# Image V in 384-column tiles, batch 0 first, with batch 1's x loaded between V's weight rows

## The chip, the cores and the metric

One core of a Trainium2 chip runs the whole program. The metric is the time of one execution on the device in microseconds (us); lower is better. "The same" means within 2% of the kernel before. All numbers below come from timed executions or from profiled ones. A profile is of a single execution.

## The reference

The program is one block of a diffusion transformer: two token streams, image and text, with joint attention. Everything is bf16.

```python
B, Ni, Nt, D = (2, 256, 32, 1152)
mod_i = (silu(c) @ wmod_img).reshape(B, 6, 1, D)      # shift, scale, gate: shi, sci, gai
hi = layernorm(x_img) * (1 + sci) + shi
qkvi = hi @ wqkv_img                                  # q, k, v of the image
# ... cut: the same for the text; joint softmax attention over 288 tokens ...
out_i = x_img + gai * (ai @ wo_img)
```

The part that matters here is the start: the layer norm of x, its transpose, the scale row `sci` (a matmul of `silu(c)` with a 2.65 MB weight), and image V. The kernel multiplies the normalized x by the scale and computes `V = (xn * (1 + sc)) @ Wv`; the shift's share of V is added later as a column.

## The kernel before

x is held as four tiles of 128 tokens: tiles 0 and 1 are batch 0, tiles 2 and 3 are batch 1. A weight of 1152 rows is held as 9 blocks of 128 rows, called rows 0 to 8 below (0.29 MB each). All these loads are issued to one DMA queue (`q1` of the page, with 39.85 of the 41.02 MB) in the order of the code. `pin` keeps an engine's instructions in program order. "Fillers" (`warm_up`) are matmuls of constants that keep TensorE busy while it waits.

```python
    ps_mm = ctx.enter_context(tc.tile_pool(name="ps_mm", bufs=6, space=PSUM))
    ps_tr = ctx.enter_context(tc.tile_pool(name="ps_tr", bufs=2, space=PSUM))

    # ... cut ...

    w_sc_i = wtile(0)
    w_v_i = wtile(1)
    sc_v, v_v = wview(wmod_img, D), wview(wqkv_img, 2 * D)
    for b in range(B):
        nc.sync.dma_start(x_i[:, b * TPB:(b + 1) * TPB, :], x_img[b].rearrange("(p t) d -> p t d", t=TPB))

    SCC = (0, 4, 7, K8, KT)
    for r0, r1 in zip(SCC, SCC[1:]):
        nc.sync.dma_start(w_sc_i[:, r0:r1, :], sc_v[:, r0:r1, :])
    for r0, r1 in ((0, 1), (1, 2), (2, 3), (3, 5), (5, 7), (7, KT)):
        nc.sync.dma_start(w_v_i[:, r0:r1, :], v_v[:, r0:r1, :])
    w_sh_i = load_w(2, wmod_img, 0)
    w_q_i = load_rows(3, wqkv_img, 0)
    w_sh_t = load_rows(0, wmod_txt, 0, (0, 1, 3, 6))
    nc.sync.dma_start(x_t[:], xt_flat[:, :])

    # ... cut ...

    xn_i = act.tile([P, NIT, D], bf, tag="A")
    hS_i = act.tile([P, KT, B * NI], bf, tag="Bt")
    xT_i = act.tile([P, KT, B * NI], bf)

    # ... cut ...

    sc_ps = ps_mm.tile([P, KT, LW], f32, tag="mm")

    def sc_rows(r0, r1):
        if r0 == 0:
            for g in range(NGG):
                mm(sc_ps[LW * g:LW * g + LW].rearrange("p c l -> p (c l)"), lhsT=unit[:], rhs=warm[:, 0:KT * LW],
                   start=True, stop=False, tile_position=(0, LW * g))
        for kt in range(r0, r1):
            for g in range(NGG):
                mm(sc_ps[LW * g:LW * g + LW], lhsT=sT32[:, kt, :], rhs=group(w_sc_i, kt, g),
                   start=False, stop=(kt == KT - 1), tile_position=(0, LW * g))

    def x_transposes(k0, b):
        tr_pool = b == 1 or k0 < 6
        tp = (ps_tr if tr_pool else ps_mm).tile([P, 3, NI], bf, tag="tr" if tr_pool else "mm", name="tp")
        for kt in range(k0, k0 + 3):
            for t in range(TPB):
                i = b * TPB + t
                tr(tp[:, kt - k0, t * P:(t + 1) * P], xn_i[:, i, kt * P:(kt + 1) * P], ident[:])
        dst = xT_i[:, k0:k0 + 3, b * NI:(b + 1) * NI]

        def copy_out():
            pin(nc.vector.tensor_copy(dst, tp[:]) if k0 == 3 else nc.scalar.copy(dst, tp[:]))

        return copy_out

    # ... cut ...

    VW = 512
    v_i = act.tile([P, NIT, D], bf, tag="A")
    accs = {}

    def v_open(ids, k0, k1, kt_major=True):
        for key in ids:
            if key not in accs:
                accs[key] = ps_mm.tile([P, VW], f32, tag="mm", name="vps")
        loop = [(kt, key) for kt in range(k0, k1) for key in ids] if kt_major else \
            [(kt, key) for key in ids for kt in range(k0, k1)]
        for kt, (i, cc) in loop:
            mm(accs[(i, cc)][:], lhsT=hS_i[:, kt, i * P:(i + 1) * P], rhs=w_v_i[:, kt, cc * VW:(cc + 1) * VW],
               start=(kt == 0), stop=(kt == KT - 1), skip_group_check=True)
            if kt == KT - 1:
                evac(v_i[:, i, cc * VW:(cc + 1) * VW], accs[(i, cc)][:])

    A0 = [(0, 0), (0, 1), (1, 0), (1, 1)]
    A1 = [(2, 0), (3, 0)]

    # ... cut ...

    s0 = ln_sums(x_i[:, 0, :], xn_i[:, 0, :])
    m1 = ln_stats(x_i[:, 1, :], P, between=silu_cols)
    ln_var(s0)
    ln_norm_dve(1, m1)
    ln_norm_act(0, s0)
    s2 = ln_sums(x_i[:, 2, :], xn_i[:, 2, :])
    m3 = ln_stats(x_i[:, 3, :], P)
    ln_var(s2)
    r3, r2 = ln_rstd(m3[:, 1:2], P), ln_rstd(s2[:, 2:3], P, sign=-1.0)
    ln_norm(x_i[:, 3, :], m3[:, 0:1], r3, P, xn_i[:, 3, :])
    ln_norm(x_i[:, 2, :], s2[:, 0:1], r2, P, xn_i[:, 2, :])
    for out in [x_transposes(k0, 0) for k0 in (0, 3, 6)]:
        out()
    sc_rows(0, 4)
    warm_up(3)
    sc_rows(4, 7)
    out01 = x_transposes(0, 1)
    out31 = x_transposes(3, 1)
    sc_rows(7, K8)
    sc_rows(K8, KT)
    out61 = x_transposes(6, 1)
    out01()
    sc_cols(0, 1)
    x_scale(0, 1, 0, step=1)
    sc_cols(1, 5)
    x_scale(1, 3, 0)
    v_open(A0, 0, 3)
    out31()
    out61()
    x_scale(0, 3, 1)
    sc_cols(5, KT)
    for k0 in (3, 6):
        for b in range(B):
            x_scale(k0, k0 + 3, b)
    v_open(A1, 0, 3)
    v_open(A0 + A1, 3, KT - 2)
    v_open(A0 + A1, KT - 2, KT, kt_major=False)

    # ... cut: mod_rows_of, 36 matmuls of 288 columns ...

    v_open([(2, 1)], 0, KT)
    p_sh = mod_rows_of(w_sh_i, sT32)
    sh_i = mod_cols_of(p_sh, "shc")
    nc.vector.tensor_copy(shT32[:, :, 0:B], sh_i[:, :, 0:B])
    # ... cut: h = xT * scale + shift in place, 18 operations on VectorE and ScalarE ...
    v_open([(3, 1)], 0, KT)

    def v_last():
        vps = ps_mm.tile([P, NIT, P], f32, tag="mm")
        for i in range(NIT):
            for kt in range(KT):
                mm(vps[:, i, :], lhsT=hS_i[:, kt, i * P:(i + 1) * P], rhs=w_v_i[:, kt, 2 * VW:D],
                   start=(kt == 0), stop=(kt == KT - 1))
        evac(v_i[:, :, 2 * VW:D], vps[:])

    # ... cut ...

    v_last()
    shift_v_rows()
    # ... cut: q and k projections, scores, softmax, attention, output projection ...
```

V is computed in tiles of 512, 512 and 128 columns. Six accumulators in PSUM, where the kernel's matmuls write their results, are open at once: four of batch 0 and two of batch 1; the rest follows later.

## Time and profile before

| | before |
|---|---|
| median of 6 runs | 118.44 us (118.32 to 118.53) |
| span of the profiled execution | 116.3 us |
| TensorE (PE) busy | 111.4 us, 96% |
| last scale row landed | 13.28 us |
| first V matmul | 14.31 us |
| first matmul of the q projection | 34.50 us |

From the profile page of the kernel before: the span, the engines' busy time, and two rows of the 40-slice table, where each digit is the busy share of one slice (2.9 us) in tenths. PEld is TensorE's weight load, DVE is VectorE, ACT is ScalarE, POOL is GpSimd.

```profile
span 116.3 us, 2500 instructions
...
PE 111.4 (96%) x1036; PEld 63.6 (55%) x1036; DVE 71.9 (62%) x151; ACT 44.9 (39%) x93; POOL 12.3 (11%) x34
...
PE   4999999999999999999999999999999999999990
...
DMA  4999999999999999999999999999999999932223
```

PE is full from the second slice to the last, and so is DMA until slice 35. Which of the two binds is told by the waits. The chain of waits of the kernel before follows the last instruction back to what released each step; columns are start in us, duration in us, and what it was.

```profile
11.15 0.75 PE wps L61 x3
11.90 0.51 PE sc_ps L61 x12
12.41 0.78 PE tp L64 x12
13.18 0.47 PE sc_ps L61 x8
...
13.68 0.23 DVE scc L257
...
14.00 0.27 DVE hS_i L264
...
14.31 13.77 PE vps L61 x63
28.08 1.22 PE gps L61 x36
29.30 4.06 PE vps L61 x45
33.36 1.22 PE gps L61 x36
34.57 19.53 PE ps L61 x90
```

Before 14.31 us PE is "busy" with fillers (`wps`) and with transposes of batch 1 (`tp`, 12 of 18 here) while the scale weights land. From 14.31 us on there is only real work, back to back: V (`vps`), the two modulation rows (`gps`), then the q projection (`ps`). From the first V matmul to the first q matmul it takes 34.50 − 14.31 = 20.19 us.

### The profile page before, as it was taken

To read this page: it belongs to the slowest core of one execution; us is meant where nothing else is said; L and a number is where in the kernel's file an instruction comes from. 1 tells how busy PE (TensorE), PEld (TensorE's weight loads), DVE (VectorE), ACT (ScalarE), POOL (GpSimd) and SP (SyncE) were. 2 spreads that over 40 slices of the span, in tenths; PEclk is the share of its full clock that TensorE was granted. 3 is DMA by queue.
4 is the path that set the end of the run, shared out by engine and by line. 5 is a ranking of instruction groups with operands and counts; after the bars stand their busy time and mean duration, and the time that the engine had idled before them with its cause. 6 is when DMAs were issued, how large, how long until landed. Compare 5 with 4: busy or idle time off the path is not lost.

```text
span 116.3 us, 2500 instructions
## 1 busy us (share of the span) xinstructions
PE 111.4 (96%) x1036; PEld 63.6 (55%) x1036; DVE 71.9 (62%) x151; ACT 44.9 (39%) x93; POOL 12.3 (11%) x34
## 2 busy tenths in 40 slices
PE   4999999999999999999999999999999999999990
PEld 1246544445574444445454457777866555666670
DVE  3468594063869999999995040017748666356671
ACT  4699710042752298825241233245747400100000
POOL 7300000000000000000000000004617000443000
PEclk9999999999999999999999999999999999999999
DMA  4999999999999999999999999999999999932223
GB/s 113 376 388 403 408 405 409 413 406 411 412 399 410 281 397 411 404 413 410 415 333 408 412 411 417 400 412 405 411 402 412 421 366 397 367 143 56 101 51 102
DMA packets 18917, 41.02 MB, mean 353 GB/s; under 512 B 1323, under 2 KB 1851, under 8 KB 18907
## 3 DMA queue, kind: packets, MB, share of 16 engines
q1 hardware_dynamic: 18032, 39.85, 89.5%
q0 software_dynamic: 480, 0.89, 2.3%
q10 hardware_dynamic: 395, 0.12, 0.4%
q8 instruction: 8, 0.13, 0.4%
q14 instruction: 2, 0.02, 0.0%
HBM read 39.52 MB, written 1.34 MB: 351 GB/s over the span
## 4 chain that ended last, share of the span: by engine, by line
PE 94%; DVE 3%; issue 0%; DVEq 0%
PE ps L61 52%; PE vps L61 15%; PE wps L61 7%; PE gps L61 5%; PE aps L61 5%; PE sps L61 5%; PE tp L64 2%; PE sc_ps L61 1%; DVE tmp L693 1%; PE pT_ps L64 1%; DVE o L694 1%; DVE warm L123 0%; PE tpt L64 0%; DVE hS_i L264 0%; DVE scc L257 0%
## 5 line engine op out<-in xcount | busy, mean ns | idle before, releaser
L61 PE MATMUL ps<-xT_i,t 128*128 128x512 bf16 x162 | 35.7, 379 | 0.0
L61 PEld LDWEIGHTS <-t 128*128 128x128 bf16 x324 | 20.5, 98 | 19.1 <-issue 0.7
L435 DVE SCALAR_TENSOR_TENSOR acc_sh<-t,sTf,acc_sh 128x1152 f32<-128x1152 bf16 x16 | 21.4, 1408 | 0.0
L61 PE MATMUL ps<-t,aT 128*128 128x384 bf16 (+3 forms) x153 | 20.3, 308 | 0.0
L61 PE MATMUL vps<-t,hS_i 128*128 128x512 bf16 (+1 forms) x108 | 17.9, 326 | 0.1
L61 PEld LDWEIGHTS <-aT 128*128 128x128 bf16 (+1 forms) x153 | 13.0, 101 | 7.1 <-issue 0.8
L61 PEld LDWEIGHTS <-hS_i 128*128 128x128 bf16 x108 | 9.0, 98 | 8.7 <-DVE hS_i L264 0.4
L365 ACT CAST qkT<-ps 128x512 bf16<-128x512 f32 (+2 forms) x11 | 6.1, 551 | 15.1 <-PE ps L61 13.7
L693 DVE TENSOR_TENSOR tmp<-ps,gb 128x384 bf16<-128x384 f32 (+2 forms) x13 | 6.8, 527 | 7.9 <-PE ps L61 7.9
L61 PE MATMUL wps<-warm 128*128 128x512 bf16 x25 | 8.7, 513 | 1.5 <-DVE unit L127 1.5
L580 POOL TENSOR_SCALAR pb<-e,rs 128x32 bf16<-128x32 f32 (+1 forms) x5 | 2.1, 414 | 74.7 <-DVE rs L577 74.6
L363 ACT ACTIVATE qkT<-ps 128x512 bf16<-128x512 f32 (+2 forms) x11 | 6.1, 561 | 8.6 <-PE ps L61 6.9
L180 DVE CAST v_i<-vps 128x512 bf16<-128x512 f32 x5 | 3.5, 692 | 7.5 <-PE vps L61 7.5
L565 DVE TENSOR_REDUCE nmx<-sps 128x1 f32<-128x288 f32 x4 | 1.8, 458 | 10.0 <-PE sps L61 10.0
L182 ACT CAST v_i<-vps 128x512 bf16<-128x512 f32 x4 | 2.3, 579 | 9.9 <-PE vps L61 9.9
L61 PEld LDWEIGHTS <-warm 128*128 128x128 bf16 x25 | 2.8, 122 | 5.8 <-issue 3.5
L61 PEld LDWEIGHTS <-sT 128*32 128x32 bf16 x180 | 4.6, 96 | 2.3 <-issue 1.6
L629 DVE TENSOR_SCALAR aT<-aps,svc 128x288 bf16<-128x288 f32 x9 | 4.3, 518 | 2.1 <-PE aps L61 2.1
L61 PE MATMUL sps<-qkT 128*128 128x288 bf16 (+1 forms) x54 | 5.5, 287 | 0.0
L61 PE MATMUL ps<-hT_t,t 128*128 128x64 bf16 x162 | 5.2, 193 | 0.1
L61 PE MATMUL gps<-t,sT 128*32 128x288 bf16 x144 | 5.2, 287 | 0.0
L61 PE MATMUL aps<-pT,v_i 128*128 128x288 bf16 x36 | 5.1, 287 | 0.0
(110 smaller groups left out, 105.3 us busy)
## 6 DMA issues: line engine op xcount, KB each, us to landing
t<-in_wqkv_txt_dram SPq DMA_DIRECT2D x3, 2592.0 KB, 19.2
t<-in_wmod_img_dram SPq DMA_DIRECT2D x2, 2592.0 KB, 14.0
t<-in_wmod_txt_dram SPq DMA_DIRECT2D x2, 2592.0 KB, 19.4
t<-in_wqkv_img_dram SPq DMA_DIRECT2D x3, 864.0 KB, 13.9
t<-in_wqkv_img_dram SPq DMA_DIRECT2D x1, 2592.0 KB
t<-in_wo_img_dram SPq DMA_DIRECT2D x3, 864.0 KB, 9.9
t<-in_wqkv_img_dram SPq DMA_DIRECT2D x3, 576.0 KB, 10.0
t<-in_wmod_txt_dram SPq DMA_DIRECT2D x2, 864.0 KB, 13.0
```

The source lines that it names most:

```text
L61: return pin(nc.tensor.matmul(*a, **k))
L64: return pin(nc.tensor.transpose(*a, **k))
L180: nc.vector.tensor_copy(out_ap, in_ap)
L182: nc.scalar.copy(out_ap, in_ap)
L363: nc.scalar.mul(out_ap, in_ap, SCALE)
L365: nc.scalar.copy(out_ap, in_ap)
L435: pin(nc.vector.scalar_tensor_tensor(acc, w_sh_t[:, kt, :], col, acc, op0=ALU.mult, op1=ALU.add))
L565: pin(nc.vector.reduce_max(nmx[0:qn, :], sps[0:qn, :], axis=AX.X, negate=True))
L580: pin(nc.gpsimd.tensor_scalar(pb[0:qn, NI + 2 * NT:NI + 3 * NT], e[0:qn, NI:NTOK], rs[0:qn, :], 0.0, op0=ALU.mult, op1=ALU.add))
L629: nc.vector.tensor_scalar(dst, tiles[(b, dt)][:], bias, None, op0=ALU.add)
L693: nc.vector.tensor_mul(tmp[:, 0:n], ps[:, 0:n], gb[:, b, c0:c0 + n])
L694: nc.vector.tensor_add(o[:, c0:c0 + n], tmp[:, 0:n], x_i[:, i, c0:c0 + n])
```

## The change

The intent: start V earlier and keep PE fed. The x of batch 1 no longer travels ahead of the scale weights, so the scale, and with it V, comes sooner. While V of batch 0 runs, batch 1's two x tiles arrive between the rows of V's weight, are normalized, and are transposed between V matmuls in two groups. The tiles of V become 384 columns wide, so that six accumulators hold exactly batch 0. In passing, the load of w_q is cut into two pieces instead of three.

The full diff:

```diff
--- before.py
+++ after.py
@@ -100,16 +100,18 @@
     w_sc_i = wtile(0)
     w_v_i = wtile(1)
     sc_v, v_v = wview(wmod_img, D), wview(wqkv_img, 2 * D)
-    for b in range(B):
-        nc.sync.dma_start(x_i[:, b * TPB:(b + 1) * TPB, :], x_img[b].rearrange("(p t) d -> p t d", t=TPB))
+    nc.sync.dma_start(x_i[:, 0:TPB, :], x_img[0].rearrange("(p t) d -> p t d", t=TPB))
 
     SCC = (0, 4, 7, K8, KT)
     for r0, r1 in zip(SCC, SCC[1:]):
         nc.sync.dma_start(w_sc_i[:, r0:r1, :], sc_v[:, r0:r1, :])
     for r0, r1 in ((0, 1), (1, 2), (2, 3), (3, 5), (5, 7), (7, KT)):
         nc.sync.dma_start(w_v_i[:, r0:r1, :], v_v[:, r0:r1, :])
+        if r0 in (1, 3):
+            i = TPB + r0 // 2
+            nc.sync.dma_start(x_i[:, i, :], x_img[1].rearrange("(p t) d -> t p d", t=TPB)[i - TPB])
     w_sh_i = load_w(2, wmod_img, 0)
-    w_q_i = load_rows(3, wqkv_img, 0)
+    w_q_i = load_rows(3, wqkv_img, 0, (0, 5))
     w_sh_t = load_rows(0, wmod_txt, 0, (0, 1, 3, 6))
     nc.sync.dma_start(x_t[:], xt_flat[:, :])
     w_k_i = load_w(4, wqkv_img, D)
@@ -211,7 +213,7 @@
     def ln_norm(x_ap, mean, rstd, np_, out_ap):
         pin(nc.vector.tensor_scalar(out_ap, x_ap, mean, rstd[0:np_, :], op0=ALU.subtract, op1=ALU.mult))
 
-    xn_i = act.tile([P, NIT, D], bf, tag="A")
+    xn_b = [act.tile([P, TPB, D], bf, tag="A%d" % b, name="xn%d" % b) for b in range(B)]
     hS_i = act.tile([P, KT, B * NI], bf, tag="Bt")
     xT_i = act.tile([P, KT, B * NI], bf)
 
@@ -225,7 +227,7 @@
         pin(nc.vector.transpose(t[:].rearrange("p c l -> p (c l)"), gps[:].rearrange("p c l -> p (c l)")))
         return t
 
-    sc_ps = ps_mm.tile([P, KT, LW], f32, tag="mm")
+    sc_ps = ps_tr.tile([P, KT, LW], f32, tag="tr")
 
     def sc_rows(r0, r1):
         if r0 == 0:
@@ -238,12 +240,10 @@
                    start=False, stop=(kt == KT - 1), tile_position=(0, LW * g))
 
     def x_transposes(k0, b):
-        tr_pool = b == 1 or k0 < 6
-        tp = (ps_tr if tr_pool else ps_mm).tile([P, 3, NI], bf, tag="tr" if tr_pool else "mm", name="tp")
+        tp = (ps_tr if b else ps_mm).tile([P, 3, NI], bf, tag="tr" if b else "mm", name="tp")
         for kt in range(k0, k0 + 3):
             for t in range(TPB):
-                i = b * TPB + t
-                tr(tp[:, kt - k0, t * P:(t + 1) * P], xn_i[:, i, kt * P:(kt + 1) * P], ident[:])
+                tr(tp[:, kt - k0, t * P:(t + 1) * P], xn_b[b][:, t, kt * P:(kt + 1) * P], ident[:])
         dst = xT_i[:, k0:k0 + 3, b * NI:(b + 1) * NI]
 
         def copy_out():
@@ -264,68 +264,67 @@
                 pin(nc.vector.tensor_scalar(hS_i[:, kt, t0:t1], xT_i[:, kt, t0:t1], sc1_i[:, kt, b:b + 1], None,
                                             op0=ALU.mult))
 
-    VW = 512
-    v_i = act.tile([P, NIT, D], bf, tag="A")
+    v_b = [act.tile([P, TPB, D], bf, tag="A%d" % b, name="v%d" % b) for b in range(B)]
     accs = {}
 
-    def v_open(ids, k0, k1, kt_major=True):
+    def v_open(ids, k0, k1, engines=None):
         for key in ids:
             if key not in accs:
-                accs[key] = ps_mm.tile([P, VW], f32, tag="mm", name="vps")
-        loop = [(kt, key) for kt in range(k0, k1) for key in ids] if kt_major else \
-            [(kt, key) for key in ids for kt in range(k0, k1)]
-        for kt, (i, cc) in loop:
-            mm(accs[(i, cc)][:], lhsT=hS_i[:, kt, i * P:(i + 1) * P], rhs=w_v_i[:, kt, cc * VW:(cc + 1) * VW],
+                accs[key] = ps_mm.tile([P, CH], f32, tag="mm", name="vps")
+        for kt, (i, cc) in [(kt, key) for kt in range(k0, k1) for key in ids]:
+            mm(accs[(i, cc)][:], lhsT=hS_i[:, kt, i * P:(i + 1) * P], rhs=w_v_i[:, kt, cc * CH:(cc + 1) * CH],
                start=(kt == 0), stop=(kt == KT - 1), skip_group_check=True)
             if kt == KT - 1:
-                evac(v_i[:, i, cc * VW:(cc + 1) * VW], accs[(i, cc)][:])
+                dst = v_b[i // TPB][:, i % TPB, cc * CH:(cc + 1) * CH]
+                if engines:
+                    pin((nc.scalar.copy if engines[ids.index((i, cc))] == "A" else nc.vector.tensor_copy)(
+                        dst, accs[(i, cc)][:]))
+                else:
+                    evac(dst, accs[(i, cc)][:])
 
-    A0 = [(0, 0), (0, 1), (1, 0), (1, 1)]
-    A1 = [(2, 0), (3, 0)]
+    V0, V1 = [[(i, cc) for i in range(b * TPB, (b + 1) * TPB) for cc in range(NCH)] for b in range(B)]
 
     def ln_norm_dve(i, mv):
-        ln_norm(x_i[:, i, :], mv[:, 0:1], ln_rstd(mv[:, 1:2], P), P, xn_i[:, i, :])
+        ln_norm(x_i[:, i, :], mv[:, 0:1], ln_rstd(mv[:, 1:2], P), P, xn_b[i // TPB][:, i % TPB, :])
 
     def ln_norm_act(i, sm):
-        ln_norm(x_i[:, i, :], sm[:, 0:1], ln_rstd(sm[:, 2:3], P, sign=-1.0), P, xn_i[:, i, :])
+        ln_norm(x_i[:, i, :], sm[:, 0:1], ln_rstd(sm[:, 2:3], P, sign=-1.0), P, xn_b[i // TPB][:, i % TPB, :])
 
-    s0 = ln_sums(x_i[:, 0, :], xn_i[:, 0, :])
+    s0 = ln_sums(x_i[:, 0, :], xn_b[0][:, 0, :])
     m1 = ln_stats(x_i[:, 1, :], P, between=silu_cols)
     ln_var(s0)
     ln_norm_dve(1, m1)
     ln_norm_act(0, s0)
-    s2 = ln_sums(x_i[:, 2, :], xn_i[:, 2, :])
-    m3 = ln_stats(x_i[:, 3, :], P)
-    ln_var(s2)
-    r3, r2 = ln_rstd(m3[:, 1:2], P), ln_rstd(s2[:, 2:3], P, sign=-1.0)
-    ln_norm(x_i[:, 3, :], m3[:, 0:1], r3, P, xn_i[:, 3, :])
-    ln_norm(x_i[:, 2, :], s2[:, 0:1], r2, P, xn_i[:, 2, :])
     for out in [x_transposes(k0, 0) for k0 in (0, 3, 6)]:
         out()
     sc_rows(0, 4)
-    warm_up(3)
     sc_rows(4, 7)
-    out01 = x_transposes(0, 1)
-    out31 = x_transposes(3, 1)
+    warm_up(1)
     sc_rows(7, K8)
+    warm_up(1)
     sc_rows(K8, KT)
-    out61 = x_transposes(6, 1)
-    out01()
     sc_cols(0, 1)
     x_scale(0, 1, 0, step=1)
     sc_cols(1, 5)
-    x_scale(1, 3, 0)
-    v_open(A0, 0, 3)
-    out31()
-    out61()
-    x_scale(0, 3, 1)
+    x_scale(1, 4, 0)
     sc_cols(5, KT)
-    for k0 in (3, 6):
-        for b in range(B):
-            x_scale(k0, k0 + 3, b)
-    v_open(A1, 0, 3)
-    v_open(A0 + A1, 3, KT - 2)
-    v_open(A0 + A1, KT - 2, KT, kt_major=False)
+    x_scale(4, KT, 0)
+    s2 = ln_sums(x_i[:, 2, :], xn_b[1][:, 0, :])
+    ln_var(s2)
+    m3 = ln_stats(x_i[:, 3, :], P)
+    r2, r3 = ln_rstd(s2[:, 2:3], P, sign=-1.0), ln_rstd(m3[:, 1:2], P)
+    ln_norm(x_i[:, 2, :], s2[:, 0:1], r2, P, xn_b[1][:, 0, :])
+    ln_norm(x_i[:, 3, :], m3[:, 0:1], r3, P, xn_b[1][:, 1, :])
+    v_open(V0, 0, K8)
+    out01, out31 = x_transposes(0, 1), x_transposes(3, 1)
+    out01()
+    out31()
+    x_scale(0, 6, 1)
+    v_open(V0[0:4], K8, KT, engines="AAVV")
+    x_transposes(6, 1)()
+    v_open(V0[4:], K8, KT, engines="AA")
+    x_scale(6, KT, 1)
+    v_open(V1[0:2], 0, KT)
 
     def mod_rows_of(w, lhs):
         gps = ps_tr.tile([P, KT, LW], f32, tag="tr")
@@ -335,7 +334,7 @@
                    start=(kt == 0), stop=(kt == KT - 1), tile_position=(0, LW * g))
         return gps
 
-    v_open([(2, 1)], 0, KT)
+    v_open(V1[2:3], 0, KT)
     p_sh = mod_rows_of(w_sh_i, sT32)
     sh_i = mod_cols_of(p_sh, "shc")
     nc.vector.tensor_copy(shT32[:, :, 0:B], sh_i[:, :, 0:B])
@@ -348,15 +347,8 @@
                                         op0=ALU.mult, op1=ALU.add)
             else:
                 nc.scalar.activation(h, h, ACT.Identity, bias=sh_i[:, kt, b:b + 1], scale=sc1_i[:, kt, b:b + 1])
-    v_open([(3, 1)], 0, KT)
-
-    def v_last():
-        vps = ps_mm.tile([P, NIT, P], f32, tag="mm")
-        for i in range(NIT):
-            for kt in range(KT):
-                mm(vps[:, i, :], lhsT=hS_i[:, kt, i * P:(i + 1) * P], rhs=w_v_i[:, kt, 2 * VW:D],
-                   start=(kt == 0), stop=(kt == KT - 1))
-        evac(v_i[:, :, 2 * VW:D], vps[:])
+    for key in V1[3:]:
+        v_open([key], 0, KT)
 
     def qk_evac(out_ap, in_ap, blk):
         if blk == 0:
@@ -539,7 +531,6 @@
                 nc.gpsimd.dma_start(gbf[r0:r0 + NT, :, :],
                                     gsc[1, b, :].rearrange("(r g j) -> g r j", r=2, g=2)[g].partition_broadcast(NT))
 
-    v_last()
     shift_v_rows()
     w_k_t = load_w(3, wqkv_txt, D)
     w_ga_i = load_w(0, wmod_img, 2 * D)
@@ -619,7 +610,7 @@
     def attn_keys(tiles, first):
         for b, dt in tiles:
             for kj in range(2):
-                mm(tiles[(b, dt)][:], lhsT=v_i[:, b * TPB + kj, dt * P:(dt + 1) * P], rhs=pTs[b][:, kj, :],
+                mm(tiles[(b, dt)][:], lhsT=v_b[b][:, kj, dt * P:(dt + 1) * P], rhs=pTs[b][:, kj, :],
                    start=(first and kj == 0), stop=(not first and kj == 1))
 
     def attn_evac(tiles):
```

More of the change, by code (lines that the diff above doesn't have):

```diff
@@ L316 @@
     sc_cols(1, 5)
-    x_scale(1, 3, 0)
-    v_open(A0, 0, 3)
-    out31()
-    out61()
-    x_scale(0, 3, 1)
-    sc_cols(5, KT)
-    for k0 in (3, 6):
-        for b in range(B):
-            x_scale(k0, k0 + 3, b)
-    v_open(A1, 0, 3)
-    v_open(A0 + A1, 3, KT - 2)
-    v_open(A0 + A1, KT - 2, KT, kt_major=False)
+    x_scale(1, 4, 0)
+    sc_cols(5, KT)
+    x_scale(4, KT, 0)
[8 more added lines that the diff above has]
+    out01()
+    out31()
+    x_scale(0, 6, 1)
[4 more added lines that the diff above has]
+    v_open(V1[0:2], 0, KT)
     def mod_rows_of(w, lhs):
```

## The prediction

> **What bounds the kernel now.** TensorE. The profile's busy table has PE at 111.4 of 116.3 us; the chain of waits is 94% PE, without a gap of note from the start of image V (14.31 us) to the last output tile. DMA is busy at 9 tenths or more until slice 35, but no PE instruction waits for it after 14 us. So only an earlier V, or less PE work after it, pays. V's start is set by DMA: the last row of the scale weights lands at 13.28 us (completion events), its matmuls start at 13.32, V 0.98 us later.
>
> **What the change does.**
>
> 1. x of batch 1 (it lands 1.36 us after batch 0's) leaves the queue ahead of the scale weights; their last row should land near 11.9 us. PE is then just the limit: transposes until 10.25, scale rows, two fillers; I count the last scale matmul at 12.1, V at 13.1. Gain 1.2 us.
> 2. The 18 transposes of batch 1 filled DMA waits before (0.06 us apart in the timeline). Now they stand between V matmuls, where PE waits for nothing: cost 1.0 us, plus 0.2 for two changes of operation.
> 3. V has 108 matmuls of 384 columns instead of 72 of 512 and 36 of 128. From 0.217 us per 512 and 0.058 per 128, V took 17.8 us; 384 columns cost 0.1625 (36 in 5.85 us in the chain, output projection): 17.55. Gain 0.2 us.
> 4. V of batch 0 eats a weight row every 0.975 us from 13.1 us on. By the bytes ahead of them, rows 3-4 should land at 16.2 and rows 5-6 at 18.3 us; needed at 16.0 and 18.2. Loss 0.1 to 0.4 us. Rows 7-8 (20.2 us) are just in time. A 16 KB instruction fetch held one DMA engine for 0.9 us at 16.2 us; if it now hits rows 5-6, 0.5 us more.
> 5. Around the transposes the copies (0.8 us on ACT, 0.55 on DVE), the multiplications (0.22 each) and the evacuations share DVE and ACT while all six accumulators are taken: 0.1 to 0.4 us on PE.
>
> **Sum at the start of the q projection** (34.50 us before): −1.2 + 1.2 − 0.2 + 0.25 + 0.25, about +0.3 us, near 34.8. What follows is the same PE sequence with the same loads, and w_q landed 1.5 us ahead of its use; the shift passes through to the end.
>
> **Prediction: 118.7 us, 118.0 to 119.5 in 8 of 10. Faster by over 2%: 0.02; within 2%: 0.94; slower by over 2%: 0.04.**
>
> **What would show each step.** Timeline: first V matmul near 13.1 us (1); transposes of batch 1 near 21 to 23 us (2); V matmuls 0.1625 us apart (3); small PE gaps at weight rows 3 and 5, ended by DMA (4); PE gaps near 23 to 25 us ended by ACT or DVE (5); first q matmul near 34.8 us, then unchanged stage lengths.
>
> **What would make it wrong.** If loads land 0.3 us earlier than I scale them, steps 4 and 5 shrink and the kernel is as much faster than before. If the layer norm of batch 1, which now starts when its x lands (14 and 17 us), ends after 21 us, or DVE's order holds copies back, PE loses up to a microsecond. [...]

One sentence, about PE's clock, is cut here. It was no term of the sum: −1.2 + 1.2 − 0.2 + 0.25 + 0.25 comes to +0.3 us as it stands.

## The result, and the profile after

| | before | after |
|---|---|---|
| median of 6 runs | 118.44 us (118.32 to 118.53) | 119.10 us (118.91 to 119.21) |
| span of the profiled execution | 116.3 us | 117.2 us |
| first V matmul | 14.31 us | 13.19 us |
| first q matmul | 34.50 us | 35.62 us |
| from V to q | 20.19 us | 22.43 us |

The ratio after to before is 1.0054 (95% interval 1.0041 to 1.0067): within 2%, clearly not faster. Ratios and intervals here use the fast runs of both kernels from the same rounds and are not quite the ratio of the medians quoted.

The timeline of PE in the profile after: start, duration, operation, count; in brackets the idle time ahead of it and what the profile holds to have ended it.

```profile
12.20 0.30 PE L61 MATMUL sc_ps<-t,sT 128*32 128x288 bf16 x4
13.19 5.05 PE L61 MATMUL vps<-t,hS_i 128*128 128x384 bf16 x30 [0.69 <-DVE hS_i L264]
19.25 3.09 PE L61 MATMUL vps<-t,hS_i 128*128 128x384 bf16 x18 [1.00 <-DVE xn L214]
22.17 0.83 PE L64 MATMUL tp<-ident,xn 128*128 128x128 bf16 x12
22.84 0.81 PE L61 MATMUL vps<-t,hS_i 128*128 128x384 bf16 x4
23.55 0.50 PE L64 MATMUL tp<-ident,xn 128*128 128x128 bf16 x6
23.88 4.88 PE L61 MATMUL vps<-t,hS_i 128*128 128x384 bf16 x29
28.69 1.29 PE L61 MATMUL gps<-t,sT 128*32 128x288 bf16 x36
29.91 4.56 PE L61 MATMUL vps<-t,hS_i 128*128 128x384 bf16 x27
34.40 1.29 PE L61 MATMUL gps<-t,shT 128*32 128x288 bf16 x36
35.62 0.60 PE L61 MATMUL ps<-xT_i,t 128*128 128x512 bf16 x2
```

V does start 1.12 us earlier. Then PE stands still after 30 V matmuls, that is after weight rows 0 to 4 (6 matmuls a row), and goes on at 19.25 us with row 5. From start to start this pair is 1.33 us apart where V matmuls are otherwise 0.163 apart: 1.17 us lost. "Busy" counts matmuls with their modelled ends, so the idle time in brackets (1.00) is smaller than the loss; gaps below are always start to start, less the usual spacing.

The pieces add up. V start: −1.12 us. The gap: +1.17 us. The 18 transposes, on PE's critical time now: +1.00 us (0.67 and 0.33 from their first start to that of the next V matmul). V itself: 17.82 us without the gap against 17.76 before, +0.06. The `gps` rows take 2.44 against 2.43. Sum: +1.12 us at the q projection, which is what the trace shows.

After that the two traces run alike: the first output projection matmul behind the text gate, at 98.82 us before, is at 99.81 us after, so 0.99 us of the 1.12 remain. The timed median shows 0.66. The profiled execution of the kernel before took 118.06 us, less than any of its six timed runs, while that after took 119.15; in later sessions the runs of before spread from 117.8 to 119.0 us. The traces thus overstate the difference by about 0.4 us. Why before spreads so was not studied.

What ended the gap? The bracket says VectorE's normalized x of batch 1 (`xn`), and so does the chain of waits of the kernel after:

```profile
9.81 6.47 DMA x_i<-in_x_img_dram
...
16.31 1.49 DVE stats L192 x3
...
18.66 0.59 DVE xn L214
19.25 3.09 PE vps L61 x18
```

But the V matmuls of row 5 read `hS_i` of batch 0 and the weight; they don't read `xn` of batch 1. The waiting matmul itself names only the semaphore of a DMA. The wait on VectorE's semaphore that the profile counted stands at the weight load ahead of it, which had run at 17.92 us. The completion events of the DMA (rows 5 and 6), which lie in the packed trace and are printed by no view of it, tell another story: 15 of its 16 parts had landed by 17.70 us, the last landed at 19.20 us, and PE went on at 19.25. That the norm ended at 19.24 us is a coincidence.

Each load has 16 completion events in this trace, as many as the page counts DMA engines; that each part is the report of one engine is inferred from that. PE went on 0.05 us after the sixteenth part here, and 0.04 us after it in three runs below (20.54 and 20.58 us, 16.86 and 16.90, 19.14 and 19.18), never after the fifteenth. Why was one part 1.50 us late? In the window from 16.7 to 17.2 us, the profile's DMA view of the kernel after shows a packet that is not data (columns: packets, MB, share of 16 engines):

```profile
q1 hardware_dynamic: 92, 0.19, 97.5%
q8 instruction: 1, 0.02, 12.0%
```

It is a fetch of 16 KB of instructions: it started at 16.92 us and took 0.96 us on one engine. There are 8 such fetches in the run, and PE has about 2070 instructions, weight loads included. The fetches are not evenly spaced (256 of PE's instructions from the first to the second, 439 from the third to the fourth). The profile tells neither for which engine a fetch was nor on which of the 16 it ran. That it was PE's, and that it held up the late part, is inferred, and the experiments below test it. The lag stayed: the last part of the shift weight, 7.7 us later, landed at 26.93 us, the others by 25.60. Why one part came 1.50 us late after a fetch of 0.96 us stays open. The kernel before has its first fetch at 16.20 us, and there too the last parts of rows 5 and 6 were late (14 of 16 by 17.71 us, then 18.31 and 18.84). It cost nothing, because V reached that row later. A fetch is not the only cause of a late part, however: in the kernel before, the last part of row 0 came at 14.00 us, 0.63 us behind the next, and no fetch had run yet in that span. The cause of this was not studied.

### The profile page after: what moved, and what is told of

The parts are those of the page before. It is cut to its first block, busy times and chain, and to the rows that moved or that the text cites. A ratio compares the mean times of both kernels' runs of the same rounds, so it can differ in the third digit from the quotient of the medians.

```text
span 117.2 us, 2498 instructions
## 1 busy us (share of the span) xinstructions
PE 110.5 (94%) x1029; PEld 65.0 (55%) x1035; DVE 71.0 (61%) x151; ACT 46.1 (39%) x96; POOL 12.3 (10%) x34
## 4 chain that ended last, share of the span: by engine, by line
PE 79%; DMA 12%; DVE 4%; SPq 1%; issue 1%; ACT 0%
PE ps L61 52%; PE vps L61 11%; DMA t<-in_wmod_img_dram 7%; DMA x_i<-in_x_img_dram 6%; PE gps L61 5%; PE aps L61 5%; PE sps L61 4%; DVE stats L192 1%; DVE tmp L684 1%; PE pT_ps L64 1%; PE tp L64 1%; DVE o L685 1%; DVE xn L214 1%; SPq L107 0%; SPq L103 0%
## 5 line engine op out<-in xcount | busy, mean ns | idle before, releaser
L61 PE MATMUL vps<-t,hS_i 128*128 128x384 bf16 x108 | 18.4, 326 | 1.7 <-DVE xn L214 1.0
L61 PEld LDWEIGHTS <-hS_i 128*128 128x128 bf16 x108 | 10.3, 98 | 8.8 <-issue 1.5
L61 PE MATMUL wps<-warm 128*128 128x512 bf16 x23 | 8.2, 518 | 1.5 <-DVE unit L129 1.5
L250 ACT COPY xT_i<-tp 128x768 bf16<-128x768 bf16 x4 | 3.1, 808 | 6.0 <-PE tp L64 6.0
L61 PE MATMUL aps<-pT,v 128*128 128x288 bf16 x36 | 5.1, 287 | 0.0
L622 ACT ACTIVATE aT<-aps,svc 128x288 bf16<-128x288 f32 x9 | 4.3, 500 | 1.4 <-PE aps L61 1.4
## 6 DMA issues: line engine op xcount, KB each, us to landing
t<-in_wqkv_img_dram SPq DMA_DIRECT2D x1, 1440.0 KB, 17.9
```

The lines of the kernel that those rows point to most:

```text
L61: return pin(nc.tensor.matmul(*a, **k))
L622: nc.scalar.activation(dst, tiles[(b, dt)][:], ACT.Identity, bias=bias)
```

## The experiments

Three theories of the gap:

- **T1**: one DMA engine is held up by TensorE's instruction fetch; the row that is being loaded then comes late, and the gap is where the fetch falls.
- **T2**: the queue order and the size of the piece (x tile 3 ahead of a piece of two rows) delay rows 5 and 6; the fetch has nothing to do with it.
- **T3**: the layer norm of batch 1 on VectorE ends the wait, as the chain says.

All experiments gave correct results. "before" beside them is the kernel before in the same rounds.

| run | first V | gaps (us, at V row) | first q | median | before | ratio (95%) |
|---|---|---|---|---|---|---|
| changed kernel | 13.19 | 1.17 (row 5) | 35.62 | 119.10 | 118.44 | 1.0054 (1.0041 to 1.0067) |
| long fillers | 12.80 | 0.25 (5), 0.69 (7) | 35.01 | 118.34 | 118.32 | 1.0007 (0.9987 to 1.0027) |
| short fillers | 13.33 | 0.63 (3), 0.13 (5) | 35.35 | 118.88 | 118.32 | 1.0041 (1.0009 to 1.0072) |
| x tile 3 later | 12.55 | 0.26 (3), 0.82 (5), 0.08 (7), 0.55 (transposes) | 35.52 | 119.05 | 118.32 | 1.0061 (1.0041 to 1.0082) |
| V in 384 alone | 14.51 | none | 34.71 | 118.51 | 118.32 | 1.0031 (0.9997 to 1.0064) |
| single rows | 12.90 | 0.42 (6) | 34.58 | 118.22 | 118.74 | 0.9974 (0.9943 to 1.0004) |
| single rows, long fillers | 12.95 | none | 34.22 | 117.84 | 118.74 | 0.9944 (0.9913 to 0.9975) |
| transposes in the gap | 12.83 | 0.02 (3), 0.21 (5) | 34.25 | 117.62 | 118.74 | 0.9927 (0.9893 to 0.9962) |
| x first | (slow profile) | | | 119.42 (fast runs alone: 119.39) | 118.74 | 1.0065 (1.0028 to 1.0102) |
| before, long fillers | 14.29 | none | 34.48 | 118.38 | 118.43 | 0.9992 (0.9969 to 1.0014) |
| no middle fillers | 12.26 | none in V, 0.21 at `gps` | 33.73 | 117.66 | 118.43 | 0.9940 (0.9912 to 0.9968) |

In the kernels with the changed order and loads, the first q matmul is the first V matmul plus 21.26 us (22.43 less 1.17, of the changed kernel) plus the gaps, to 0.01 us: long fillers 12.80 + 0.94 + 21.26 = 35.00; x tile 3 later 12.55 + 1.71 + 21.26 = 35.52; single rows 12.90 + 0.42 + 21.26 = 34.58. The one exception is "transposes in the gap", which orders PE's work otherwise (34.32 by this sum, 34.25 measured). So the gaps are the whole of what differs, besides the start.

The start itself is no longer set by a DMA: it varies from 12.55 to 13.33 us among runs whose last scale row landed alike (11.20 to 11.27 us in these two and in the changed kernel). V follows PE instead: it starts 0.99 to 1.00 us after the first of the last four scale matmuls (12.20 and 13.19 us in the changed kernel, 11.81 and 12.80 with long fillers, 12.34 and 13.33 with short ones, 11.90 and 12.90 with single rows). The early PE work does not keep one pace: in the changed kernel's trace the fillers are 0.426 us apart until 6.8 us and 0.216 apart from 7.2 us on; in the trace of the kernel before, 0.427 until 7.2 and 0.216 from 7.5 us on. So this switch fell about 0.4 us apart in two executions. The granted clock reads 1.00 in all these stretches; what sets the switch is not shown, and that the varying start comes from it is my guess.

### Long fillers: fewer instructions ahead of V

```diff
     nc.vector.memset(warm[:], 1.0)
+    warm32 = const.tile([P, 512], f32)
+    nc.gpsimd.memset(warm32[:], 1.0)
@@
-    warm_up(8)
+    def warm_up_long(n):
+        for _ in range(n):
+            mm(wps[:], lhsT=warm32[:, 0:P], rhs=warm32[:], start=True, stop=True)
+
+    warm_up_long(2)
@@
-    warm_up(14)
+    warm_up_long(3)
+    warm_up(1)
```

> The changed kernel with its 22 fillers at the start replaced by 5 [...]f32 ones and 1 bf16: about as long, but 40 TensorE instructions fewer ahead of V, so TensorE's first 16 KB instruction fetch comes about 20 V matmuls (3.3 us) later, near 20 us instead of 16.92. Theory T1 (the gap of 1.33 us ahead of weight row 5 is one DMA engine held up by that fetch, 15 of 16 engines had landed by 17.70 us): rows 5-6 land whole by 17.8 us, the gap shrinks to 0.2 us or less, the q projection starts near 34.5 us instead of 35.62, time 118.0 to 118.3. Theory T2 (queue order and the size of the piece delay rows 5-6, whatever the fetch does): gap 1.0 to 1.3 us, time 119.0. Theory T3 (the layer norm of batch 1 on VectorE, which the chain of waits names as the releaser): norm at the same time, gap unchanged, time 119.0.

Measured: an f32 matmul is recorded as two matmuls, each with its own weight load, so only 22 TensorE instructions were saved (1018 matmuls instead of 1029, and 11 weight loads fewer), not 40. The fetch moved from 16.92 to 18.17 us, as the DMA view of the window 17.9 to 18.4 us of this run shows:

```profile
q1 hardware_dynamic: 92, 0.20, 102.8%
q8 instruction: 1, 0.02, 12.0%
```

Rows 5 and 6 now landed whole at 17.91 us, and the gap ahead of them fell from 1.17 to 0.25 us. The late engine showed on rows 7 and 8 instead: 15 parts by 19.34 us, the last at 20.54. The PE timeline of this run:

```profile
12.80 7.25 PE L61 MATMUL vps<-t,hS_i 128*128 128x384 bf16 x42 [0.69 <-DVE hS_i L271]
20.58 1.14 PE L61 MATMUL vps<-t,hS_i 128*128 128x384 bf16 x6 [0.52 <-DMA t<-in_wqkv_img_dram]
```

42 matmuls are rows 0 to 6; row 7 waits, and the profile now names the DMA. The gap went where the fetch went. T2 and T3 expected it to stay at row 5 near 1.1 us, and it did not. In this trace V also started 0.39 us earlier, but with row 5's last part at 19.20 us, as in the changed kernel, that alone would only have lengthened the wait. T1's size was missed: I expected the fetch past all of V's rows and a time of 118.0 to 118.3; it fell on the last of them, and the time was 118.34 us, equal to before.

### Short fillers: more instructions ahead of V

```diff
-    warm_up(14)
+    for _ in range(28):
+        mm(wps[:, 0:256], lhsT=warm[:, 0:P], rhs=warm[:, 0:256], start=True, stop=True)
```

> The changed kernel with the 14 second fillers cut into 28 of half the width: 28 TensorE instructions more ahead of V, so the first instruction fetch comes 14 V matmuls (2.3 us) earlier, near 14.6 us. T1: the late engine now hits rows 3-4 (others by 15.6 us, it near 17.0), the gap moves to row 3 (needed at 16.1), about 0.9 us, and no more than 0.3 us are left at row 5; time 118.8 to 119.2. T2 and T3: gap stays at row 5 with 1.1 to 1.3 us; time 119.1.

Measured: the fetch started at 14.10 us. Rows 3 and 4 landed on 15 engines by 15.57 us and on the last at 16.86. The PE timeline of this run:

```profile
13.33 3.10 PE L61 MATMUL vps<-t,hS_i 128*128 128x384 bf16 x18 [0.69 <-DVE hS_i L265]
16.90 5.17 PE L61 MATMUL vps<-t,hS_i 128*128 128x384 bf16 x30 [0.47 <-DMA t<-in_wqkv_img_dram]
```

18 matmuls are rows 0 to 2: the gap (0.63 us) is at row 3, with 0.13 us more at row 5. With the fetch at 14.1, 16.9 and 18.2 us the main gap was at rows 3, 5 and 7. That fits T1 (which engine was late is still inferred) and refutes T2 and T3 as the main cause: in the changed kernel, 15 of the 16 parts had landed 0.38 us before row 5 could have run (17.70 against 18.08 us), so the whole wait was for the last part. Order and size still have a part, as two runs below show: with x tile 3 later, rows 5 and 6 came 0.73 us sooner, and with single rows the gap was 0.42 instead of 1.17 us.

### x tile 3 later: its order alone

```diff
-        if r0 in (1, 3):
-            i = TPB + r0 // 2
+        if r0 in (1, 5):
+            i = TPB + r0 // 4
```

> The changed kernel with the second x tile of batch 1 issued behind weight rows 5-6 instead of behind rows 3-4. T1: rows 5-6 have 0.72 us less ahead of them; 15 engines by 17.0 us, the late one near 18.4, needed at 18.1: gap near 0.5 instead of 1.33, time 118.4. T2: no gap at all, time 118.0. T3: the norm runs 0.7 to 1.4 us later, the gap grows to about 2 us, time 119.8.

Measured: 119.05 us, no gain; none of the three was right in size. Rows 5 and 6 came 0.73 us sooner, as T1 had it (15 parts by 17.19, the last at 18.47), but V also started 0.64 us sooner in this execution, so the gap was still 0.82 us. And x tile 3 was now the late one, at 19.11 us. The timeline of this run, all engines:

```profile
19.13 1.48 DVE L192 BATCH_NORM_STATS2 stats<-x_i 128x6 f32<-128x384 bf16 x3 [2.72 <-DMA x_i<-in_x_img_dram]
...
21.48 0.58 DVE L214 TENSOR_SCALAR xn<-x_i,mv,rstd 128x1152 bf16<-128x1152 bf16 x1 [0.17 <-ACT rstd L210]
...
22.12 0.79 PE L64 MATMUL tp<-ident,xn 128*128 128x128 bf16 x11 [0.39 <-DVE xn L214]
```

Here the transposes do read `xn`, and PE waits 0.55 us for the norm. From its landing to the end of the norm an x tile takes 2.95 us (19.11 to 22.06), so it can't be put off further: the gap turned into a new wait.

### V in 384 columns alone, on the kernel before

The kernel before with its own loads and transposes; only V's tiles, their order and the order of VectorE's scale operations were changed. The core of the edit:

```diff
-    VW = 512
+    VW = CH
@@
-    v_open(A0, 0, 3)
+    v_open(V0, 0, 3)
@@
-    v_open(A1, 0, 3)
-    v_open(A0 + A1, 3, KT - 2)
-    v_open(A0 + A1, KT - 2, KT, kt_major=False)
+    v_open(V0, 3, KT - 2)
+    v_open(V0, KT - 2, KT, kt_major=False)
+    v_open(V1[0:2], 0, KT)
@@
-    v_last()
```

> The kernel before with its own loads and its own places for the transposes, but V in 384-column tiles, batch 0 first. Matmul time alone: 108 at 0.1625 us are 17.55 us against 17.76 from first V matmul to the end before, so 0.1 to 0.2 us shorter; V starts at 14.31 as before, every row has landed when it is needed (row 5 needed at 19.2, landed 18.84), no gap: 118.25 to 118.4. If narrow tiles or their order were a cost of their own in the changed kernel: slower than before, 118.6 or more.

Measured: 118.51 us against 118.32, ratio 1.0031 with an interval that holds 1: no difference is shown, and so not the gain that was expected. The PE timeline of this run:

```profile
14.51 13.34 PE L61 MATMUL vps<-t,hS_i 128*128 128x384 bf16 x81
```

The next operation started at 27.78 us. These 13.27 us and 4.49 us for the other 27 matmuls make 17.76 us, exactly what V takes before (13.70 + 4.06). The narrower tiles gain nothing and lose nothing on PE. No row was waited for, because V starts later here.

### Single rows: finer pieces

```diff
-    for r0, r1 in ((0, 1), (1, 2), (2, 3), (3, 5), (5, 7), (7, KT)):
+    for r0, r1 in [(r, r + 1) for r in range(KT)]:
         nc.sync.dma_start(w_v_i[:, r0:r1, :], v_v[:, r0:r1, :])
-        if r0 in (1, 3):
-            i = TPB + r0 // 2
+        if r0 in (1, 4):
+            i = TPB + r0 // 3
```

> The changed kernel with weight rows 3 to 8 of V in single-row loads instead of pairs (x tiles in the same places, before row 2 and before row 5). If the loss is a wait for the last of 16 DMA engines on a two-row piece: row 5 lands near 18.5 us by the late engine, row 6 near 19.2; gap of 0.4 us at row 5 instead of 1.2 us in excess, q projection near 34.9 us, time 118.3 to 118.6. If the piece size does not matter and only total bytes do: gap 1.1, time 119.0.

Measured: 118.22 us (118.11 to 118.26). Row 5 landed on time at 17.14 us; the fetch at 16.83 us made row 6 late (15 parts by 17.83, the last at 19.14). The gap was 0.42 us, at row 6 rather than at row 5:

```profile
12.90 6.02 PE L61 MATMUL vps<-t,hS_i 128*128 128x384 bf16 x36 [0.69 <-DVE hS_i L264]
19.18 2.11 PE L61 MATMUL vps<-t,hS_i 128*128 128x384 bf16 x12 [0.25 <-DMA t<-in_wqkv_img_dram]
```

In the changed kernel rows 5 and 6 were one piece, and row 5 began at 19.25 us, after the late part of both (19.20). Here PE did row 5 in that time, and only row 6 waited for the late part.

### Single rows and long fillers

The two edits above together.

> Single-row loads and long fillers together. Late engine from about 18.2 us on: row 7 lands near 19.8 us and is needed near 19.7, row 8 20.5 and 20.7: gaps of 0.2 us in all. First V matmul to q projection then is pure TensorE time, 21.3 us (22.43 less 1.17); with V at 12.8 to 13.2 us q starts at 34.1 to 34.5 us: time 117.9 to 118.3, equal to before or a little faster. If some other cost were left, q later than 34.7 us.

Measured: 117.84 us against 118.74 of before in the same rounds, ratio 0.9944; q at 34.22 us, no gap at any row. V's 48 matmuls of rows 0 to 7 run through:

```profile
12.95 7.97 PE L61 MATMUL vps<-t,hS_i 128*128 128x384 bf16 x48 [0.69 <-DVE hS_i L271]
20.77 0.83 PE L64 MATMUL tp<-ident,xn 128*128 128x128 bf16 x12
```

This is the changed kernel without its wait. It beats before, but only by the difference of two large terms: it starts 1.36 us earlier and takes 1.08 us longer from V to q.

### Transposes in the gap

Long fillers, the loads as in the changed kernel, and:

```diff
-    v_open(V0, 0, K8)
+    v_open(V0, 0, K8 - 1)
     out01, out31 = x_transposes(0, 1), x_transposes(3, 1)
+    v_open(V0, K8 - 1, K8)
```

> Long fillers, loads as in the changed kernel, and 12 of the 18 transposes of batch 1 put ahead of weight row 7, where the run with long fillers waited 0.69 us for its load. If a transpose costs time only where TensorE would not have waited: the wait takes up 0.67 us of transposes, q projection near 34.4 us instead of 35.01, time 117.7 to 117.9 against 118.34 of that run. If the transposes pay their time wherever they stand: 118.3.

Measured: 117.62 us (117.54 to 117.91), q at 34.25 us. The last part of rows 7 and 8 landed at 20.29 us, later than row 7 could have run, but PE was busy with transposes until 20.56:

```profile
12.83 7.22 PE L61 MATMUL vps<-t,hS_i 128*128 128x384 bf16 x42 [0.69 <-DVE hS_i L271]
19.89 0.83 PE L64 MATMUL tp<-ident,xn 128*128 128x128 bf16 x12
20.56 1.79 PE L61 MATMUL vps<-t,hS_i 128*128 128x384 bf16 x10
```

Without the transposes there, PE would have waited for row 7 from 19.89 to about 20.33 us (an estimate: the landing plus the 0.05 us seen above). So some 0.4 of their 0.67 us cost nothing in this execution, rather than all of it. Against long fillers, q is 0.76 us earlier: the wait of 0.69 us at row 7 is gone, and the rest are small differences. The kernel before put all 18 transposes into such waits.

### x first: the loads of before in the changed kernel

```diff
-    nc.sync.dma_start(x_i[:, 0:TPB, :], x_img[0].rearrange("(p t) d -> p t d", t=TPB))
+    for b in range(B):
+        nc.sync.dma_start(x_i[:, b * TPB:(b + 1) * TPB, :], x_img[b].rearrange("(p t) d -> p t d", t=TPB))
@@
-        if r0 in (1, 3):
-            i = TPB + r0 // 2
-            nc.sync.dma_start(x_i[:, i, :], x_img[1].rearrange("(p t) d -> t p d", t=TPB)[i - TPB])
```

> The changed kernel with the x loads of before (both batches ahead of the scale weights). V starts at 14.3 to 14.5 us, all weight rows have landed when needed, no gap; from V to q 21.3 us because the transposes still stand between V matmuls: q near 35.7 us, time 119.0 to 119.3, as slow as the changed kernel. So the load order gains 1.1 us and loses it again in the gap. If the load order were a net gain, slower than 119.5; if a net loss, faster than 118.8.

Measured: 119.39 us in the fast runs (119.42 with the slow one), ratio 1.0065 (the changed kernel: 1.0054). The time fits the expectation that the changed load order gains in the start about what it loses in the gap. But the profile fell in a slow execution (120.77 us), so its stages are not compared here; what the fast ones look like, and so this account of the time, is not shown.

### Control: the kernel before with long fillers

The same edit of the fillers, on the kernel before.

> Control: the kernel before with the long fillers. Its V starts when the last scale row lands (13.3 us) plus 0.98 us, whatever the fillers do, and every V row has landed long before it is needed, so a later first instruction fetch has nothing to save: ratio to before 0.998 to 1.002. If the long fillers by themselves made a kernel faster (clock, issue), ratio 0.996 or less, and the gain of the runs with long fillers would not be due to the fetch.

Measured: ratio 0.9992 (0.9969 to 1.0014), V at 14.29 us, q at 34.48 us. The fetch moved here too, from 16.20 to 17.24 us. So the long fillers are not faster as such in this kernel. The control can't tell what they do to the start of V where PE sets it, as in the changed kernel (12.80 to 12.95 us in three traces with them, 12.55 to 13.33 us in four with bf16 fillers). Their gain there is put down to the moved fetch because an earlier start alone would only have lengthened the wait for row 5.

### No middle fillers

Single rows and long fillers, without the two bf16 fillers between the last scale rows:

```diff
-    warm_up(1)
     sc_rows(7, K8)
-    warm_up(1)
     sc_rows(K8, KT)
```

> Single-row loads and long fillers, without the two bf16 fillers between the last scale rows: the last scale matmul can follow its row (11.5 us) instead of 12.0 us, so V starts near 12.5 us instead of 12.95 and q near 33.9 instead of 34.2 us: time 117.5 against 117.84. If the weight rows then arrive too late, gaps come back at rows 2 to 5 (row 5 lands near 17.4 us, needed at 17.35) and the time stays 117.8. [...]

Measured: V at 12.26 us, q at 33.73 us in its profile (an execution of 117.42 us), median 117.66 us (117.37 to 118.49), ratio 0.9940. The trace shows the 0.5 us sooner that was expected, but the runs spread more and the ratio is that of single rows with long fillers (0.9944): a gain of its own is not shown. V ran without a gap; a new, small one stood ahead of the first modulation rows (`gps`, 0.21 us). Both kernels are beaten by three versions, all by less than 1%.

## Why the prediction was right, and where its sum was off

The time, 119.1 us, lies inside the range of 118.0 to 119.5 us, and the class, within 2%, was right. The mechanism was right: an earlier start, paid back by transposes on PE and by late weight rows. The size of one term was not. Point by point, from the traces:

1. Earlier start: −1.2 predicted, −1.12 measured. The last scale row landed at 11.22 us (11.9 predicted), but PE was the limit, as predicted: the last scale matmul was at 12.20 (12.1), V at 13.19 (13.1).
2. and 3. Transposes and the change of tiles: +1.2 and −0.2, so +1.0 predicted; +1.06 measured. The split was off: the tiles gained nothing (V alone in 384 columns took 17.76 us, as before), and the changes of operation cost less than 0.2.
4. **The mis-sized term**: "Loss 0.1 to 0.4 us", entered in the sum as +0.25. It measured 1.17 us, all at row 5; without the late part it would have been nothing, as the other 15 parts landed by 17.70 us (18.3 predicted). The prediction had named the reason as a possibility ("if it now hits rows 5-6, 0.5 us more"), but the fetch did hit, and one part came 1.50 us behind the others, not 0.5. I had scaled from before, where the last part was 0.53 us behind the next one, and not asked whether the fetch could be worse. Behind the first 14 parts it was 1.13 us late even there (17.71 and 18.84 us), close to what then came. The gap that it expected at row 3 was not there: that piece landed at 15.56 us, not at 16.2.
5. Waits for VectorE and ScalarE around the transposes: +0.25 predicted. The V matmuls there kept their spacing but for changes of operation: 0.

The sum at the q projection was predicted as +0.3 us and is +1.12 in the traces. The missed term (0.92 too little) and the waits that didn't come (0.25 too much) make up most of the difference. The prediction of the time came closer (+0.3 against +0.66) because the profiled execution of before was one of its fastest, while the timed runs were slower. That part is luck.

After the 0.69 us of idle PE ahead of V in the changed kernel, V's matmuls were 0.163 us apart from the second on, and the granted clock was 1.00 from 13.19 to 18.20 us. In the slow execution of x first the granted clock was 0.56 from 14.10 to 18.00 us, where V starts; one slow execution settles nothing about the cause.

## What to carry to other kernels

An earlier start is worth only what the later critical work does not take back: here the start gained 1.1 us and moved 1.0 us of transposes from a wait, where they were free, into the middle of a stage that never waits. A stage that starts earlier also meets its loads with less slack: look at the last of the 16 completions (here 19.20 us, the others by 17.70), not at the mean landing, and try loading what is consumed row by row in single rows (here the gap fell from 1.17 to 0.42 us). When the releaser that a profile names feeds data that the waiting instruction does not read, look for the true one among the completions that came at the same moment.
